# A routed two-layer MoE after attention: one ranking phase moved ahead of an expert, later ranking products moved two places on

## The chip, the cores and the metric

The kernel runs on one core of a Trainium2 chip. The metric is the device time of one execution in microseconds (us). The core has a matrix engine (TensorE, PE in the rows, with its weight loads as PEld), a vector engine (DVE), an activation engine (ACT), GpSimd (POOL) and SyncE (SP), which here mostly issues the weight transfers. Each engine works through its own instructions in program order and waits for the others through semaphores.

## The reference, cut to what matters

Attention over 2 batches, 8 heads and 576 positions gives 1152 rows of 512. They go through a first MoE with 8 experts (top 1, gated), and its output through a second one with 8 experts of exactly 144 rows each. The second is assigned greedily over all logits:

```python
def _moe2_ref(x, w_gate, w1, w2):
    N, D = x.shape
    E = w_gate.shape[1]
    cap = N // E
    logits = x @ w_gate
    flat = logits.flatten()
    order = np.argsort(-flat)
    assigned = -np.ones(N, dtype=np.int64)
    counts = np.zeros(E, dtype=np.int64)
    for idx in order:
        tok, e = (int(idx) // E, int(idx) % E)
        if assigned[tok] >= 0 or counts[e] >= cap:
            continue
        assigned[tok] = e
        counts[e] += 1
    out = np.zeros((N, D), dtype=np.float32)
    for e in range(E):
        mask = assigned == e
        h = np.maximum(x[mask] @ w1[e], 0.0)
        out[mask] = h @ w2[e]
    return out
```

In the attention, the score rows have a maximum subtracted before the exponential. That changes nothing but the range of the numbers.

## The kernel before, in words

**Attention.** A loop over `m` works on one head per turn, several stages of different heads side by side. `ORDER` is a hand-written list of stage names, one list for even and one for odd turns, and sets the order on every engine. `M0` to `M3` make the score pieces from which the row maxima come, `D0` to `D3` take the maxima on DVE (line 488, tile `rm`), `G0` rounds them on ACT (`q_dve0`, line 494), and `G1` uses them on POOL. `TE` copies transposed operands on ACT (line 409), `E0` to `E3` end in the exponentials on ACT (line 536), and `S` and `QS` split operands.

**Experts.** The weights of 16 experts (8 of each MoE) come from HBM in quarters of a 2 MB matrix, issued by SP (line 128) as soon as the expert is known and its buffer is free. Most of them are split into a high f16 part on ACT (line 160) and a low bf16 part on DVE (line 164), so that a product is three matmuls of 16 bit. The layers of the second MoE are `layer1` (lines 1004 to 1006) and `second2` (line 1948). For the second layer, `HALF2` says how many of the 8 row chunks are split; the rest are multiplied as f32. e8 to e15 are the experts of the second MoE in the order in which they fill up.

**Ranking.** That order comes from ranking phases. Phase 0 runs over all rows; phases 1 to 7 (`phases`, a generator) over the rows that are left. A phase puts the maxima into rows by PE transposes (`rows_of`, line 1221) and ACT copies (line 1224), compares on DVE (line 1661) and ACT (line 1659) into tiles `g`, multiplies these on PE (line 1667, behind the start on line 1845), takes from that the rows of the expert that has filled up (`mx`, `BA`, `own`, `O`, `R` on DVE), counts on PE (line 1885), and gets the expert's number into `evi`. `known` makes SP load that number and start the expert's weights. Then `slot_pe` (line 1518) and `choose` give the row numbers `tok`, with which POOL gathers the rows (`xg`, line 1523); `spread` transposes them (line 1543) into `xt`, the expert's input.

**What sets the order there.** `moe2` calls `tick(k)` at 22 places of an expert's two layers, k from 0 to 11 in the first and 12 to 21 in the second, and a script says for each place what goes in: `w` the next step of the ranking, `h` and `l` a high and a low part of the weights that come next, `s` and `t` the two halves of the next spread, `0` and `1` the transposes and output of the expert before (`back2`, line 1964). `FIRST` is e8's script, `THEN` that of all others. Ahead of e8, phase 1 is begun: rows, three steps of compares. `warm(n)` issues n matmuls of 512 columns whose result nobody reads (line 1721).

Of the kernel before, what the change touches and what calls it, by code (L numbers as in the profile page):

```python
# [14 lines left out]
OP = mybir.AluOpType  # L15
AX = mybir.AxisListType
# [5 lines left out]
def tile_attention_moe_moe(ctx: ExitStack, tc: tile.TileContext, q, k, v, s, wg1, w1a, w2a, capacity,  # L22
# [94 lines left out]
    def load_part(i, c):  # L117
        w, k = halves[i]
        t = loaded[i] = place(i)
        e = order[i // 2]  # L120
        src = (w[e:e + 1] if isinstance(e, int) else w[bass.ds(e, 1)]).rearrange("o (c p) f -> p (o c) f", p=P)
        n, f = src.shape[1:]
        t = t.rearrange("p (c f) -> p c f", c=n)
        if i // 2 == E:
            sl = (slice(None), slice(None), slice(c * f // 4, (c + 1) * f // 4))
        else:
            sl = (slice(None), slice(c * n // 4, (c + 1) * n // 4))
        nc.sync.dma_start(t[sl], src[sl])
# [45 lines left out]


    HALF2 = 4
    second_splits = [(2 * E + i, part) for i in range(2 * E) for part in range(HALF2 // 2 if i % 2 else 4) if i != 1]

    def split_next():
        if split_queue:  # L180
# [634 lines left out]
    def some_w(n):  # L815
# [4 lines left out]
    between = gate0()  # L820

    ORDER = [
        "E0 Q E1 K X1 M0 D0 V0 M1 V1 D1 X QE M2 VS XE E3 P0 D2 P1 QS E2 V2 R0 R1 G0 M3 T R2 D3 XG VT TE L LG G1 LV S".split(),
        "E0 VS M0 V0 Q D0 M1 E1 D1 P0 P1 V1 X1 E3 K E2 QE M2 V2 D2 R0 M3 X T R1 G0 LG XE TE R2 D3 QS L S G1 VT XG LV".split(),
    ]
    made = {}
    for m in range(-7, NH + 3):
# [700 lines left out]

    gates = []

    def spread(xg, x=None, k=None, between=(0, 0)):
        if not k:
            gates.append(rw.tile([S2, 2], F32, name="gq", bufs=3))
            nc.vector.tensor_copy(gates[-1], xg[:, :, DM + E])
        x16 = xg.bitcast(F16)
        x = x or mo2["xt"].tile([P, 8, CAP2], F16, name="xt")
        ks = range(2) if k is None else (k,)
        prs = {k: banks[k].tile([P, 512], F32).bitcast(F16)[:, :4 * CAP2].rearrange("p (c q) -> p c q", c=4)
               for k in ks}
        for h in range(2):  # L1540
            for k in ks:
                for c in range(4):
                    nc.tensor.transpose(prs[k][:, c, h * S2:(h + 1) * S2],
                                        x16[:, h, (4 * k + c) * P:(4 * k + c + 1) * P], ident[:S2, :S2])
            if between[h]:
                warm(between[h])
        for k in ks:
            (nc.vector.tensor_copy if k else nc.scalar.copy)(x[:, 4 * k:4 * k + 4], prs[k])
        return x
# [143 lines left out]
    def pop_lo():  # L1693
        if late:
            split_lo(*late.pop(0))
# [142 lines left out]
    def phases():  # L1838
# [3 lines left out]
        for p in range(1, E):  # L1842
# [29 lines left out]
            own = rw.tile([P, CT, E], F32, name="own1")  # L1872
            r = rw.tile([P, CT], F32, name="r1")
            nw = rw.tile([P, CT], F32, name="nw1")
            nc.vector.tensor_tensor(own, pc, BA, OP.mult)
            if not last:
                nc.vector.reduce_sum(nw, BA, axis=AX.X)
            nc.vector.reduce_sum(r, own, axis=AX.X)
            O, R, places = slot_ones(r, BA, Lr[:, :, E], CT, 1)
            in_turn(places)  # L1880
            nc.gpsimd.tensor_add(SL2, SL2, own)
            nc.gpsimd.tensor_add(A, A, BA)
            yield
            for t in range(CT):
                nc.tensor.matmul(cnt2, ones, BA[:, t], start=t == 0, stop=t == CT - 1)
            f, ops = newly_full(p)
# [3 lines left out]
            if not last:  # L1890
# [2 lines left out]
                                                               op0=OP.mult, op1=OP.add),  # L1893
                        lambda: nc.vector.tensor_scalar(pen, fp, -BIG, None, op0=OP.mult),
                        lambda: nc.vector.tensor_tensor(Lo, Lo, c3(pen), OP.add)] + ops
            in_turn(counts, [None] + left)
            known(p)
            if not last:
                m, Bo, Bh, tm = new
            yield  # L1900
# [2 lines left out]
            in_turn(choose(p, f))  # L1903
            chosen.append(p)
            yield

    chk = rp.tile([P, 2, NTT, E], F32, name="chk")
    bad = rp.tile([P, 2, E + 1], F32, name="bad")
# [79 lines left out]
    def moe2(script, first=False):  # L1988
        pend = None
        given.difference_update(range(E, 2 * E))  # L1990
        for e in range(E):
# [21 lines left out]
                    load_next()  # L2013
                    gather_next()

            halved = HALF2 if e else 0
            hs = layer1(mo2, split_ws(i0), XT1.pop(e), CAP2, none, tick, halved)
            pend = (e, second2(i0 + 1, hs, halved, tick), gates[0])
            gates.pop(0)
# [20 lines left out]

    FIRST = "w . lw . . w . w w w w . w . wh l w h st lh wl hll"
    THEN = "w h l h l0 w w . w . h w1l h wl h . w l s tl h l"
    FIRST, THEN = (x.split() for x in (FIRST, THEN))
    next(work)
    pop_lo()
    pop_lo()
    pop_hi()
    warm(WARM2[2])  # L2050
    XT1[0] = spread(xg.pop(0), between=(3, 2))
    next(work)
    next(work)
    next(work)
    pop_hi()
    pop_lo()
    moe2(lambda e, k: (THEN if e else FIRST)[k].strip("."), True)
    assert next(work, None) is None
    bv = nc.values_load(badi[0:1, 0:1], min_val=0, max_val=4 * E)
    with tc.If(bv > 0):  # L2060
        with tc.If(nc.values_load(overi[0:1, E:E + 1], min_val=0, max_val=1) > 0):
            overflown()
        route_all()
        split_queue += second_splits
        given.difference_update(range(E, 2 * E))
        loads += [(i, c) for i in range(2 * E, 4 * E) for c in range(4)]
        order.update({E + e: e for e in range(E)})
        load_next()
        late.clear()
        for _ in range(3):  # L2070
            pop_hi()
        pop_lo()
        XT1[0] = spread(gather(tok[:, 0]))

        def again(e, k):
            if k == 8 and e + 1 < E:
                xg[e + 1] = gather(tok[:, e + 1])
            return THEN[k].strip(".")

        moe2(again)  # L2080
    last_rows()
# [35 lines left out]
```

## Time and profile before

| what | value |
|---|---|
| three executions | 442.37, 442.89 (median), 448.96 us |
| profiled execution | 441.93 us, of which the span of instructions is 440.1 us |
| granted TensorE clock, mean over the span | 0.973 of full |
| busy in the span | PE 396.0, PEld 366.0, DVE 333.6, ACT 261.8, POOL 191.1 us |
| HBM read | 81.42 MB |

Times of rows count from the span's start. The profiled execution is 1.83 us longer than its span, and 0.96 us shorter than the median. A matmul's row is longer than its turn on the engine, since matmuls overlap: its cost is read from start to start.

### The profile page before, as it was taken

The numbers are of one execution on the slowest core, as the hardware profiler recorded it, in microseconds if no ns is written. First come the engines' busy times: TensorE is split into PE (matmuls) and PEld (weight loads), VectorE is DVE, ScalarE is ACT, GpSimd is POOL, SyncE is SP. The second block draws the span as 40 slices with busy tenths as digits, with TensorE's granted clock in tenths as the row PEclk, the third lists the DMA queues.
The fourth block names the chain that finished last, engine by engine and source line by source line (L and its number), as shares of the span: only waits on it lengthen the run. The fifth ranks groups of instructions, "written<-read, shape, count | busy, mean of one in ns | idle before, by whom it ended". The sixth has DMA issues, their size and how long they took to land.

```text
span 440.1 us, 13965 instructions
## 1 busy us (share of the span) xinstructions
PE 396.0 (90%) x5376; PEld 366.0 (83%) x5376; DVE 333.6 (76%) x955; ACT 261.8 (59%) x472; POOL 191.1 (43%) x306
## 2 busy tenths in 40 slices
PE   1679999998878799999999999869989999999994
PEld 1457888886766799999999999738879999999993
DVE  7889999989677377867778894858596878876730
ACT  4448888876482255556565853535476776766641
POOL 4397788875770702142044181522054244244121
PEclk9979999999899999999999999988989999999998
DMA  6797899952987869999999691188999697899511
GB/s 153 168 216 166 181 212 225 224 148 81 311 290 234 298 158 306 384 343 343 335 346 391 99 174 20 29 251 218 356 359 343 200 354 281 242 334 345 171 41 35
DMA packets 94399, 103.04 MB, mean 234 GB/s; under 512 B 56136, under 2 KB 63304, under 8 KB 94323
## 3 DMA queue, kind: packets, MB, share of 16 engines
q1 hardware_dynamic: 88931, 91.85, 71.6%
q0 software_dynamic: 4192, 9.91, 7.3%
q8 instruction: 44, 0.72, 0.7%
q10 hardware_dynamic: 1200, 0.30, 0.3%
q14 instruction: 32, 0.26, 0.2%
HBM read 81.42 MB, written 14.59 MB: 218 GB/s over the span
## 4 chain that ended last, share of the span: by engine, by line
PE 57%; DMA 14%; DVE 13%; issue 6%; ACT 4%; SPq 3%; POOL 2%; POOLq 0%; DVEq 0%; ACTq 0%
PE C L1061 11%; DMA xg<-x2d,tok 7%; PE A L1004 4%; PE A L1005 4%; PE A L1006 4%; PE pog L559 3%; PE C L1948 3%; PE pT L452 3%; DVE wl L164 3%; PE pM L476 2%; PE pE L528 2%; DMA wf<-in_moe_w_dram 2%; PE pE L529 2%; DVE wf L164 2%; PE A L1948 2%
## 5 line engine op out<-in xcount | busy, mean ns | idle before, releaser
L164 DVE TENSOR_TENSOR wl<-wf,wh 128x1024 bf16<-128x1024 f32 x64 | 77.0, 1222 | 22.7 <-ACT wh L160 22.2
L160 ACT ACTIVATE wh<-wf 128x1024 f16<-128x1024 f32 x64 | 65.7, 1050 | 18.5 <-DMA wf<-in_moe_w_dram 10.5
L1005 PE MATMUL A<-xt,wh 128*128 128x144 f16 (+4 forms) x288 | 59.5, 231 | 0.0
L1006 PE MATMUL A<-xt,wl 128*128 128x144 f16 (+4 forms) x288 | 59.5, 231 | 0.0
L1004 PE MATMUL A<-xt,wh 128*128 128x144 f16 (+4 forms) x288 | 59.5, 231 | 0.0
L1061 PE MATMUL C<-h,wf 128*128 128x160 f32 (+7 forms) x544 | 58.3, 269 | 0.0
L1176 POOL DMA_INDIRECT x2d<-xo,tix x14 | 22.9, 1638 | 71.2 <-DVE l L1193 26.5
L1004 PEld LDWEIGHTS <-wh 128*128 128x128 f16 x512 | 50.6, 99 | 2.2 <-PE pM L653 1.6
L1005 PEld LDWEIGHTS <-wh 128*128 128x128 f16 x512 | 50.4, 99 | 1.5 <-issue 1.0
L1006 PEld LDWEIGHTS <-wl 128*128 128x128 bf16 x512 | 50.5, 99 | 0.0
L536 ACT ACTIVATE pf<-pE,XB 128x512 f32<-128x512 f32 (+4 forms) x80 | 36.9, 514 | 10.5 <-PE pE L531 10.3
L414 POOL TENSOR_TENSOR pl<-pf,ph 128x512 f16<-128x512 f32 x30 | 35.6, 1196 | 11.4 <-DVE ph L403 8.8
L1972 POOL DMA_INDIRECT out_dram<-x2f,tok x14 | 16.2, 1160 | 55.4 <-ACT h L1012 26.3
L164 DVE TENSOR_TENSOR wf<-wf,wf 128x1024 bf16<-128x1024 f32 x30 | 35.7, 1218 | 2.6 <-ACT wf L160 2.6
L1523 POOL DMA_INDIRECT xg<-x2d,tok x16 | 24.9, 1556 | 26.3 <-PE A L1221 11.2
L1061 PEld LDWEIGHTS C<-h,wf 128*128 128x128 f32 x256 | 36.2, 190 | 0.0
L488 DVE CUSTOM_DVE_ANT_0 junk<-pM,cb 128x128 f16<-128x128 f32 (+4 forms) x80 | 32.1, 430 | 4.6 <-PE pM L478 3.9
L476 PE MATMUL pM<-al,ar 128*128 128x128 f16 (+2 forms) x96 | 26.5, 317 | 7.1 <-DVE rm L488 6.9
L1948 PE MATMUL C<-h,wf 128*128 128x144 f32 (+1 forms) x312 | 32.6, 260 | 0.0
L160 ACT ACTIVATE wf<-wf 128x1024 f16<-128x1024 f32 x30 | 31.3, 1051 | 0.0
L559 PE MATMUL pog<-vf,pf 128*128 128x65 f32 x180 | 29.1, 284 | 0.0
L1006 PE MATMUL C<-xt,wl 128*128 128x144 f16 x128 | 25.1, 229 | 0.0
(431 smaller groups left out, 1190.0 us busy)
## 6 DMA issues: line engine op xcount, KB each, us to landing
wf<-in_moe_w_dram SPq DMA_DIRECT2D x128, 512.0 KB
xd<-zero SPq DMA_DIRECT2D x18, 257.0 KB
cb<-cumd SPq DMA_DIRECT2D x16, 288.0 KB
x2d<-zero SPq DMA_DIRECT2D x9, 260.5 KB
kf<-in_k_dram SPq DMA_DIRECT2D x16, 128.0 KB
vf<-in_v_dram SPq DMA_DIRECT2D x16, 128.0 KB
qf<-in_q_dram SPq DMA_DIRECT2D x14, 128.0 KB
bl<-al SPq DMA_DIRECT2D x16, 72.0 KB
```

The costliest lines, as they stand in the source:

```text
L160: nc.scalar.activation(hi, src, AF.Copy)
L164: nc.vector.tensor_sub(lo, src, hi)
L414: (nc.gpsimd if ENG[name][i % 2] == "P" else nc.vector).tensor_sub(o, x, y)
L476: nc.tensor.matmul(o, AR[m][:, t * P:(t + 1) * P], AL[m][:, j0:j1], start=True, stop=not diag)
L488: nc.vector.tensor_tensor_reduce(junk[:w, :j1 - j0], o, CB[m][:w, j0:j1], 1.0, r if t == 4 and j0 == 0 else -3e38, OP.add, OP.max, r)
L536: nc.scalar.activation(d, o, AF.Exp, bias=x, scale=2.0 ** -13)
L559: nc.tensor.matmul(o, pf[:, c:c + P], VF[n % 4][:, j, h], start=False, stop=j == t)
L1004: nc.tensor.matmul(ph[:, g], wh[:, c, fs], xt[:, c], start=c == 0, stop=False)
L1005: nc.tensor.matmul(ph[:, g], wh[:, c, fs], xt[:, 4 + c], start=False, stop=False)
L1006: nc.tensor.matmul(ph[:, g], wl[:, c, fs], xt[:, c], start=False, stop=c == 3)
L1061: nc.tensor.matmul(py[:, g], a[:, f, d], b[:, f], start=k == 0, stop=k == len(terms) - 1)
L1948: nc.tensor.matmul(py[:, g], a[:, f, d], b[:, f], start=k == 0, stop=k == len(terms) - 1)
```

## The change

There are five edits.

- In `ORDER`, `G0` goes behind `D3` (and, on even turns, behind `TE`): the maxima are rounded when the last piece is in.
- Phase 1 is carried further ahead of e8's first layer: its products run between the two halves of e8's spread, its count behind them, and `known(1)` ahead of the layer. Its `choose` comes at place 5 of e8, and what prepares phase 2 (`left`) at place 6 instead of together with the count. The matmuls of `warm` around it are 2 and 2 instead of 3 and 2.
- The scripts: e8's phase 2 compares at places 11 and 12 and multiplies at 14 (before: 8 to 10 and 12). e9 has a script of its own, `SECOND`. In `THEN` the products stand at place 10 instead of 8, the count at 13 instead of 11, `choose` at 16 instead of 13, and the next rows at 20 instead of 16.
- e8's second weight matrix is loaded in blocks of rows (128x2x512) instead of blocks of columns (128x8x128).
- e9's second layer isn't split any more: `halved` is 0 for it, as for e8, and its two pieces leave the list of splits.

```diff
-        if i // 2 == E:
+        if i == 2 * E:
             sl = (slice(None), slice(None), slice(c * f // 4, (c + 1) * f // 4))
...
-    second_splits = [(2 * E + i, part) for i in range(2 * E) for part in range(HALF2 // 2 if i % 2 else 4) if i != 1]
+    second_splits = [(2 * E + i, part) for i in range(2 * E) for part in range(HALF2 // 2 if i % 2 else 4) if i not in (1, 3)]
...
-        "E0 Q E1 K X1 M0 D0 V0 M1 V1 D1 X QE M2 VS XE E3 P0 D2 P1 QS E2 V2 R0 R1 G0 M3 T R2 D3 XG VT TE L LG G1 LV S".split(),
-        "E0 VS M0 V0 Q D0 M1 E1 D1 P0 P1 V1 X1 E3 K E2 QE M2 V2 D2 R0 M3 X T R1 G0 LG XE TE R2 D3 QS L S G1 VT XG LV".split(),
+        "E0 Q E1 K X1 M0 D0 V0 M1 V1 D1 X QE M2 VS XE E3 P0 D2 P1 QS E2 V2 R0 R1 M3 T R2 D3 XG VT TE G0 L LG G1 LV S".split(),
+        "E0 VS M0 V0 Q D0 M1 E1 D1 P0 P1 V1 X1 E3 K E2 QE M2 V2 D2 R0 M3 X T R1 LG XE TE R2 D3 G0 QS L S G1 VT XG LV".split(),
...
             if between[h]:
-                warm(between[h])
+                between[h]()
...
-            in_turn(places)
-            nc.gpsimd.tensor_add(SL2, SL2, own)
-            nc.gpsimd.tensor_add(A, A, BA)
-            yield
+            if p == 1:
+                yield
+            else:
+                in_turn(ranked)
+                in_turn(places)
+                kept_ranks()
+                yield
             for t in range(CT):
                 nc.tensor.matmul(cnt2, ones, BA[:, t], start=t == 0, stop=t == CT - 1)
...
-            in_turn(counts, [None] + left)
-            known(p)
+            if p == 1:
+                yield
+                in_turn(counts, ranked)
+                known(p)
+                yield
+                in_turn(places)
+                kept_ranks()
+            else:
+                in_turn(counts, [None] + left)
+                known(p)
...
+            if p == 1:
+                in_turn(left)
+                yield
...
-            halved = HALF2 if e else 0
+            halved = HALF2 if e > 1 else 0
...
-    FIRST = "w . lw . . w . w w w w . w . wh l w h st lh wl hll"
-    THEN = "w h l h l0 w w . w . h w1l h wl h . w l s tl h l"
+    FIRST = "w . l . . w w . . . . www w . wh l h w st wlh wl hll"
+    SECOND = ". . . . 0 w w w . . w 1 h wl h . wl h ls tl wh l"
+    THEN = "w h l h l0 w w . . . wh 1l h wl h . w l s tl wh l"
...
     next(work)
     pop_lo()
     pop_lo()
     pop_hi()
+    for _ in range(3):
+        next(work)
+    pop_lo()
+    pop_hi()
     warm(WARM2[2])
-    XT1[0] = spread(xg.pop(0), between=(3, 2))
+
+    def ranked_first():
+        next(work)
+        warm(2)
+
+    def counted_first():
+        next(work)
+        warm(2)
+
+    XT1[0] = spread(xg.pop(0), between=(ranked_first, counted_first))
     next(work)
-    next(work)
-    next(work)
-    pop_hi()
-    pop_lo()
```

Three places show the moves on an engine. The first is DVE between e8's second and third low part (`wl_84`) and phase 1's maximum `mx`, `BA` and number `evi`; `gq` and `xt` belong to e8's spread, `tot` is the count. Before:

```order
L1504 TENSOR_TENSOR R_5797<-BA_5787,hq_5795 128x40 x2
L164 TENSOR_TENSOR wl_84<-wf_78,wh_83 128x4x256
L1888 TENSOR_TENSOR tot<-tot,px 128x8
L1676 TENSOR_SCALAR full<-tot 128x8
L1892 SCALAR_TENSOR_TENSOR Lm<-nw_5791,Lm 128x5
```

After:

```order
L1871 SCALAR_TENSOR_TENSOR BA_5756<-mx_5754,Bo_5674 128x40
L1548 COPY xt<-A_5715 128x576
L1895 TENSOR_TENSOR tot<-tot,px 128x8
L1875 TENSOR_TENSOR own_5758<-px,BA_5756 128x40
L1676 TENSOR_SCALAR full<-tot 128x8
L1876 TENSOR_REDUCE nw_5760<-BA_5756 128x5
```

The count and the number now stand ahead of the slot tiles `O` and `R` and of e8's fourth low part, not behind them.

The second place is DVE in e8's second layer, behind phase 2's slot tile `R`; `wl_86` is the first low part of e9's first matrix. Before:

```order
L1504 TENSOR_TENSOR R_6036<-BA_6026,hq_6034 128x40 x2
L1888 TENSOR_TENSOR tot<-tot,px 128x8
L1676 TENSOR_SCALAR full<-tot 128x8
L1892 SCALAR_TENSOR_TENSOR Lm<-nw_6030,Lm 128x5
L1677 TENSOR_TENSOR nf<-full 128x8
```

After:

```order
L1504 TENSOR_TENSOR R_6040<-BA_6033,hq_6038 128x40 x2
L164 TENSOR_TENSOR wl_86<-wf_3046,wh_85 128x4x256
L1895 TENSOR_TENSOR tot<-tot,px 128x8
L1676 TENSOR_SCALAR full<-tot 128x8
L1899 SCALAR_TENSOR_TENSOR Lm<-nw_6037,Lm 128x5
```

Phase 2's count, and with it e10's number, now stands behind a split of e9's weights.

The third place is ACT in one attention turn, with the rounding of `rm`, the copies `al` and `ar` of `TE`, and the exponentials `pf` of the next turn. Before:

```order
L494 ACTIVATE rm_159<-rm_159,magic 128x5
L409 ACTIVATE al_140<-pT 128x576
L409 ACTIVATE ar_146<-pT 128x576
L536 ACTIVATE pf_161<-pE,XB 128x512
L536 ACTIVATE pf_161<-pE,XB 128x64
```

After:

```order
L409 ACTIVATE al_140<-pT 128x576
L409 ACTIVATE ar_146<-pT 128x576
L494 ACTIVATE rm_159<-rm_159,magic 128x5
L536 ACTIVATE pf_161<-pE,XB 128x512
L536 ACTIVATE pf_161<-pE,XB 128x64
```

The rounding went from ahead of the two copies to right ahead of the exponentials, and it now waits for the maximum of the last piece.

## Rows read from the trace of the kernel before

**Rows 1.** The page, chain that ended last, by engine.

```profile
PE 57%; DMA 14%; DVE 13%; issue 6%; ACT 4%; SPq 3%; POOL 2%; POOLq 0%; DVEq 0%; ACTq 0%
```

**Rows 2.** The chain in order of time, 280 to 440: start, us, what.

```profile
290.81 4.86 DMA xg<-x2d,tok
295.71 0.43 PE A L1543 x8
296.14 0.65 PE C L1721 x3
...
303.56 0.31 PE px L1518 x5
...
305.38 0.56 PE A L1221 x5
...
307.68 7.46 DMA wf<-in_moe_w_dram
315.25 1.06 ACT wh L160
...
346.96 0.47 PE D L1964 x4
```

**Rows 3.** Timeline of PE, e8 to e11: start, us, line, op, tiles, count.

```profile
297.65 0.28 PE L1004 MATMUL D<-xt,wh 128*128 128x144 f16 x1
...
308.29 0.18 PE L1845 MATMUL px<-tm,part 128*128 128x40 f16 x1
...
309.05 0.37 PE L1948 MATMUL D<-h,wf 128*128 128x144 f32 x1
...
312.45 0.37 PE L1948 MATMUL C<-h,wf 128*128 128x144 f32 x1
...
314.50 0.20 PE L1543 MATMUL A<-ident,xg 72*128 72x72 f16 x1
...
319.01 0.23 PE L1004 MATMUL C<-xt,wh 128*128 128x144 f16 x1
...
338.95 0.23 PE L1004 MATMUL D<-xt,wh 128*128 128x144 f16 x1
...
341.95 0.27 PE L1964 MATMUL D<-identf,y 128*72 128x128 f32 x1
...
343.89 0.18 PE L1845 MATMUL px<-tm,part 128*128 128x40 f16 x1
...
345.19 0.22 PE L1004 MATMUL A<-xt,wh 128*128 128x144 f16 x1
...
355.65 0.23 PE L1004 MATMUL C<-xt,wh 128*128 128x144 f16 x1
```

**Rows 4.** Timeline of DVE, in attention and in e8.

```profile
66.20 0.07 DVE L488 DVE_READ_ACCUMULATOR2_ANT rm<- 64x1 f32 x1
...
105.28 0.07 DVE L488 DVE_READ_ACCUMULATOR2_ANT rm<- 64x1 f32 x1
...
304.15 0.15 DVE L1679 TENSOR_SCALAR evi<-evf 128x1 int32<-128x1 f32 x1
```

**Rows 5.** Windows: stretch, length; busy of PE, PEld, DVE, ACT, POOL; PEclk, DMA, GB/s.

```profile
40.00:65.00 25.00, 25.00 (x367) 21.58 (x366) 24.24 (x86) 20.99 (x49) 19.84 (x25) 1.00 0.89 187
...
293.50:297.00 3.50, 1.29 (x20) 0.93 (x21) 0.73 (x2) 0.94 (x2) 0.29 (x4) 0.98 0.48 117
297.00:300.50 3.50, 3.50 (x52) 2.99 (x49) 3.35 (x7) 2.99 (x4) 0.00 (x0) 0.51 1.16 311
300.50:302.50 2.00, 2.00 (x38) 2.00 (x36) 1.90 (x12) 0.41 (x1) 0.49 (x2) 1.00 1.17 295
```

**Rows 6.** Timeline of ACT in attention; in brackets its idle time before and what ended it.

```profile
64.75 0.30 ACT L494 ACTIVATE rm<-rm,magic 128x5 f32<-128x5 f32 x1
...
66.14 1.42 ACT L536 ACTIVATE pf<-pE,XB 128x512 f32<-128x512 f32 x3
...
107.64 0.65 ACT L409 ACTIVATE xt<-pT 128x576 f16<-128x576 f16 x1 [2.91 <-PE pT L452]
```

More of the change, by code (lines that the diff above doesn't have):

```diff
@@ L1529, in tile_attention_moe_moe, with spread @@
     gates = []
-    def spread(xg, x=None, k=None, between=(0, 0)):
+    def spread(xg, x=None, k=None, between=(None, None)):
         if not k:
@@ L1874, in phases, with kept_ranks @@
             nw = rw.tile([P, CT], F32, name="nw1")
[L1875 to L1878, printed above, removed]
+            ranked = [lambda: nc.vector.tensor_tensor(own, pc, BA, OP.mult),
+                      lambda: last or nc.vector.reduce_sum(nw, BA, axis=AX.X),
+                      lambda: nc.vector.reduce_sum(r, own, axis=AX.X)]
             O, R, places = slot_ones(r, BA, Lr[:, :, E], CT, 1)
-            in_turn(places)
-            nc.gpsimd.tensor_add(SL2, SL2, own)
-            nc.gpsimd.tensor_add(A, A, BA)
-            yield
+            def kept_ranks():
+                nc.gpsimd.tensor_add(SL2, SL2, own)
+                nc.gpsimd.tensor_add(A, A, BA)
+            if p == 1:
[5 more added lines that the diff above has]
+                yield
             for t in range(CT):
@@ L2039, in gather_next @@
                 passed(999)
-    FIRST = "w . lw . . w . w w w w . w . wh l w h st lh wl hll"
-    THEN = "w h l h l0 w w . w . h w1l h wl h . w l s tl h l"
-    FIRST, THEN = (x.split() for x in (FIRST, THEN))
+    FIRST = "w . l . . w w . . . . www w . wh l h w st wlh wl hll"
+    SECOND = ". . . . 0 w w w . . w 1 h wl h . wl h ls tl wh l"
+    THEN = "w h l h l0 w w . . . wh 1l h wl h . w l s tl wh l"
+    SCRIPTS = [x.split() for x in [FIRST, SECOND] + [THEN] * (E - 2)]
     next(work)
@@ L2049, in tile_attention_moe_moe @@
     pop_hi()
+    for _ in range(3):
+        next(work)
+    pop_lo()
+    pop_hi()
     warm(WARM2[2])
-    XT1[0] = spread(xg.pop(0), between=(3, 2))
-    next(work)
-    next(work)
-    next(work)
-    pop_hi()
-    pop_lo()
-    moe2(lambda e, k: (THEN if e else FIRST)[k].strip("."), True)
+    def ranked_first():
[5 more added lines that the diff above has]
+    XT1[0] = spread(xg.pop(0), between=(ranked_first, counted_first))
+    next(work)
+    moe2(lambda e, k: SCRIPTS[e][k].strip("."), True)
     assert next(work, None) is None
@@ L2077, in again @@
                 xg[e + 1] = gather(tok[:, e + 1])
[L2078 removed]
+            return SCRIPTS[-1][k].strip(".")
         moe2(again)
```

## The prediction

> **What bounds the kernel now.** I read the chain of waits first. PE has 57% of it [rows 1], so most of the span is matmuls in sequence, and only a stretch whose chain runs through something else can give much. The reader is to look for such a stretch, and it lies between 290 and 327: the chain goes from e8's gather (the rows land at 290.81 + 4.86 = 295.67) through e8's transposes and small matmuls to a weight transfer of 7.46 us, and then to e9's first high part on ACT at 315.25 [rows 2]. e9's weights are loaded only when phase 1 has found e9, and they come too late.
>
> The timeline of PE gives the price. First layers start at 297.65 (e8), 319.01 (e9), 338.95 (e10) and 355.65 (e11) [rows 3]: an expert takes 21.36, 19.94 and 16.70 us. The chain runs through PE from e10 on, so 16.70 is what PE needs, and the first two are longer by waits. DVE's timeline has e9's number `evi` at 304.15 [rows 4]; the weights are in at 315.15, 11.0 us behind it.
>
> **The change part by part.**
>
> *Phase 1 ahead of e8.* All of phase 1's products, its count and four warming matmuls now stand between e8's gather and e8's first layer; the compares run while PE waits for the gather anyway, so they cost nothing. The prices: eight transposes 0.43; the products from 308.29 to 309.05, 0.76; a warming matmul 0.65 / 3 = 0.22 [rows 2, 3]. The granted clock matters here. The windows show it at 0.98 in 293.5 to 297, when PE was busy for only 1.29 of 3.5 us, then 0.51 up to 300.5, and 1.00 behind that [rows 5]: half rate came behind the wait for the gather and ended while e8's first layer ran. The wait stays, so I take the same times. Then: 295.71 + 0.43 + 0.76 = 296.9; two warming matmuls at half rate 0.87; the other eight transposes 0.43; the count, five matmuls of 8 columns, 0.31 as the like step on line 1518 [rows 2]; two more 0.87. e8's first layer starts at about 299.4, **1.75 later** (at full rate throughout it would be 298.2, 0.55 later).
>
> The trace can't show what the transposes themselves do for the clock, since warming matmuls ran beside them. The Trainium skill (TensorE: Matmul & The Clock Gate, Part 4: PE-mode transpose) says that transposes in that mode don't count as activity for the clock in the way matmuls do. By that rule e8's new start, with fewer warming matmuls and no layer beside the ranking, would stay at half rate for longer, and the sum would be that of the second rival; by the rows it is the one here.
>
> *e8 itself.* I build it from e10's 16.70. In e10 the ranking takes from 343.89 to 345.19, 1.30 where the products alone take 0.76, so 0.54 is a wait for ACT's compares. A whole f32 second layer is 64 half products of (314.50 - 312.45) / 16 = 0.128, 8.2 us. A half split one is 48 products of (341.95 - 338.95) / 48 = 0.0625 and 32 of 0.128, 7.1 us [rows 3]. So an f32 expert without waits is 16.70 - 0.54 + 1.1 = 17.26. e8 has no transposes of an expert before it (2 x 0.47) but a second slot step and a second rows step (0.31 + 0.56) [rows 2], which cancel. The clock is at half until 300.5 [rows 5], 1.1 us of e8, which costs 0.55. e8: 17.8 instead of 21.36, so e9 starts at 317.2, **1.85 earlier**.
>
> What must hold for that: phase 2's products come behind 12 f32 products of e8's second layer (24 halves, 3.1 us), when both compares are done. And e8's second matrix must be in by about 306.5; its rows of 2 KB were asked for at the same time as the columns before, which the f32 products got without a wait. Row blocks I cost at nothing for that reason. If they came later than 306.5, each us would count in full, since the first product now needs all four quarters soon.
>
> *e9's weights.* The number is now some eight small DVE steps (about 0.15 each, as `evi`'s 0.15 [rows 4]) behind the count, near 299.8 instead of 304.15. With the 11.0 us of before, the weights are in at 310.8. Queued behind them: e9's first low part stands on DVE ahead of phase 2's count, and that ahead of e10's number and of the next rows. Phase 2's products end near 310.7 and the slot tiles some 2 us later, so the weights have about 1 us of slack there. The three other splits then fit into the end of e8 and e9's first layer, where each quarter takes PE 1.5 us and a split less.
>
> *e9's second layer in f32* costs PE 1.1 us (above) and takes two high and two low parts off ACT and DVE, which today stand between the compares of phase 3. With weights in time and the products behind the first layer, no wait is left: e9 takes 17.26 instead of 19.94, **2.7 less**. e10 starts at 334.4.
>
> *Products two places later* in e10, e11 and e12: the wait of 0.54 goes in each, **1.6 less**. e13's phase has no compares. The next expert's number comes later in its expert by two places, some 2 us; in e11 the weights have over 3 us between landing and first use, so I cost this at nothing. POOL's gather and SP's load stand behind the same steps and also move by some 2 us with nearly an expert's time to spare.
>
> *Rounding behind D3.* In attention PE is busy 25.0 of 25 us and DVE 24.24 [rows 5]. On ACT the rounding is 0.30 long and the exponentials start at 66.14 [rows 6]; the last maximum is ready at 66.27 [rows 4], so they start at about 66.6, 0.46 later, and on the other turns about 0.30. ACT is busy 20.99 of 25 and has an idle gap in each turn, so I take **nothing**; without this cover it is 0.3 to 0.46 per head. It may be below nothing too, because D3 no longer waits for the rounding.
>
> **The sum**: -1.85 - 2.7 - 1.6 = -6.15. Against the profiled execution, 441.93 - 6.15 = 435.8. The median lies 0.96 above that execution, so I expect a median of about **436.5**.
>
> **The rivals.**
>
> *First: e9 is known early, but its weights aren't there early*, because they queue behind e8's second matrix and the gather. For it: the transfers were near full from 297 on (DMA share 1.16 and 1.17 [rows 5]). Against it: the first expert's transfer was through before e9's was asked for. If they land at 315.15 as before, the first split ends near 317.5, phase 2's count and the next rows follow on DVE, and e9 starts near 320, 1.0 later than before; e9 and the ranking still gain 2.7 + 1.6. That is 441.93 - 3.3 = 438.6, or 439.5 as a median.
>
> *Second: the clock.* If all of e8's first layer ran at half rate, its 96 x 0.0625 = 6.0 us would cost 6.0 more instead of 0.55: 441.93 - 0.7 = 441.2, a median of 442, no change. Against it: PE is nearly without pause from 295.7, as it was when the clock came back in the trace.
>
> *Third, on the slower side: the rounding holds ACT.* It waits for D3 in ACT's queue, and the next turn's exponentials stand behind it. With no cover that is 8 x 0.46 + 8 x 0.30 = 6.1 us. Near the end it is more: D3 is ready only at 105.35 [rows 4], and the idle 2.91 before the copy at 107.64 [rows 6] shows what cover there is; twice that is 5.8. In all up to 11.9, so 441.93 - 6.15 + 11.9 = 447.7. It decides against the change once more than half of that (6.15) reaches PE. The chain through attention has PE in nearly every step, which speaks against it.
>
> *Fourth, better:* full rate sooner at e8 (1.2 + 0.55), D3 free of its wait, a little less elsewhere: 8 to 9 us, a median near 434.
>
> **How the numbers follow.** Forecast (434 to 438.5) 0.58; first rival 0.16; second 0.08; third 0.06; fourth 0.12. The range from 432.8 to 441.8 takes in the fourth, the first and part of the second. Two per cent, about what a measurement of this kernel can tell from no change, is 434.0 and 451.7. Half to all of the fourth lies below 434.0, hence faster 0.12; only a bad third rival reaches 451.7, hence slower 0.04; the same 0.84.
>
> **What would show each step.** In the changed profile: e8's first layer near 299.4, e9's near 317.2, e10's near 334.4, then steps of 16.2; `evi` near 299.8; no wait of ACT for e9's weights beyond 311; half clock ending by 300.5; attention as long as before. I am wrong if e8's start moves by more than 3 us, if e9's first split waits for its transfer beyond 313, or if ACT's wait for D3 turns up as a wait of PE.

## The result, and the profile after

The changed kernel takes **438.75 us** (median of 20 executions, 436.99 to 443.77), the kernel before beside it 443.4 (20 executions, 441.87 to 448.96): a ratio of **0.9892, 95% interval 0.9868 to 0.9916**, 4.65 us less. That is 1.1%, less than the 2% that the prediction took for a clear difference. Forecast were 436.5 and a range of 432.8 to 441.8. One long execution of each kernel (443.77 and 448.96) is left out of the ratio.

The profiled execution of after took 438.96 us with a span of 437.1 and a mean granted clock of 0.970. The timeline of PE has the same first layers as before [rows 3], and a wait in e11's products:

```profile
299.48 0.33 PE L1004 MATMUL D<-xt,wh 128*128 128x144 f16 x1
...
317.56 0.23 PE L1004 MATMUL C<-xt,wh 128*128 128x144 f16 x1
...
334.74 0.23 PE L1004 MATMUL D<-xt,wh 128*128 128x144 f16 x1
...
351.39 0.23 PE L1004 MATMUL C<-xt,wh 128*128 128x144 f16 x1
...
358.21 0.27 PE L1667 MATMUL px<-Bh,g 128*128 128x8 f16 x5
358.84 0.28 PE L1667 MATMUL px<-Bo,g 128*128 128x8 f16 x5 [0.36 <-DVE g L1661]
```

e8, e9, e10 and e11 start 1.83 us later, 1.45, 4.21 and 4.26 us earlier than before. Up to e10 that is the forecast (299.4, 317.2 and 334.4). From there on nothing more is gained.

DVE has the number of e9 at 299.92 (before: 304.15 [rows 4]), and ACT splits e9's first weights at 310.46 without a wait (before: 315.25 [rows 2]). Later in the program, in e13, ACT waits for weights, and a hidden piece `h` queued behind that, and PE for the piece:

```profile
299.92 0.15 DVE L1679 TENSOR_SCALAR evi<-evf 128x1 int32<-128x1 f32 x1
```

```profile
310.46 1.04 ACT L160 ACTIVATE wh<-wf 128x1024 f16<-128x1024 f32 x1
...
391.76 1.06 ACT L160 ACTIVATE wh<-wf 128x1024 f16<-128x1024 f32 x1 [1.93 <-DMA wf<-in_moe_w_dram]
392.72 0.39 ACT L1015 ACTIVATE h<-C 128x288 f32<-128x288 f32 x1
```

```profile
393.17 0.76 PE L1966 MATMUL C<-h,wf 128*128 128x144 f32 x4 [0.39 <-ACT h L1015]
```

The windows of [rows 5] in after:

```profile
40.00:65.00 25.00, 25.00 (x369) 21.57 (x367) 24.33 (x85) 21.30 (x49) 18.31 (x24) 1.00 0.88 183
293.50:297.00 3.50, 1.12 (x31) 1.12 (x32) 3.41 (x6) 3.50 (x5) 0.49 (x4) 0.50 0.53 148
297.00:300.50 3.50, 3.50 (x39) 2.40 (x37) 2.10 (x16) 0.67 (x2) 0.50 (x2) 0.50 0.96 349
300.50:302.50 2.00, 2.00 (x26) 2.00 (x24) 1.86 (x5) 0.25 (x1) 0.00 (x0) 0.70 1.01 341
```

The clock is at half already in the wait for the gather (before: 0.98), and until behind 300.5.

For all kernels of this study the same marks, read from PE's timeline, stand in one table: from the first transpose of e8's spread (the gather has landed) to e8's first layer ("to e8"), then from each expert's first layer to the next, and the whole from the spread to e15. The stages ahead of the spread vary by some us from run to run, as said below, so profiles are compared from there. The names in the first column are runs; a bare e8 to e15 is always an expert.

```
                    to e8   e8     e9     e10    e11    e12    e13    e14   whole
before               1.94  21.36  19.94  16.70  16.70  16.16  15.00  14.97  122.77
after                3.60  18.08  17.18  16.65  16.67  16.12  15.76  15.25  119.31
e11_changed          3.31  17.49  17.18  16.66  16.67  16.12  15.11  17.07  119.61
e1_phase1_inside     1.95  21.27  17.18  16.67  16.66  16.12  15.12  15.20  120.17
e2_old_places        3.34  17.76  18.66  18.13  16.71  16.15  15.01  15.67  121.43
e3_rows_earlier      3.28  18.75  17.35  16.63  16.11  16.02  15.00  16.43  119.57
e4_old_rounding      3.59  18.15  17.17  16.67  16.67  16.12  15.12  16.53  120.02
e5_columns           3.60  18.00  17.18  16.66  16.66  16.12  15.11  16.37  119.70
e6_e9_split          3.48  18.24  18.26  16.93  16.46  16.11  15.12  15.20  119.80
e7_warm_gather       2.48  17.00  17.18  16.66  16.66  16.12  15.11  14.97  116.18
e8_rows_count        3.59  18.76  17.17  16.14  16.14  15.64  15.15  14.97  117.56
e9_best              2.48  18.58  17.86  17.00  16.14  15.64  15.15  16.86  119.71
e10_best_inside      1.94  21.44  17.18  16.54  16.14  15.64  15.15  15.23  119.26
e12_count_later      2.65  18.26  17.18  16.76  16.91  17.40  16.17  16.25  121.58
```

### The profile page after: what moved, and what is told of

It is laid out like the page before. It is cut to its first block, busy times and chain, and to the rows that moved or that the text cites. A ratio compares the mean times of both kernels' runs of the same rounds, so it can differ in the third digit from the quotient of the medians.

```text
span 437.1 us, 13916 instructions
## 1 busy us (share of the span) xinstructions
PE 394.2 (90%) x5359; PEld 364.2 (83%) x5359; DVE 327.0 (75%) x951; ACT 258.4 (59%) x470; POOL 185.9 (43%) x306
## 4 chain that ended last, share of the span: by engine, by line
PE 57%; DMA 14%; DVE 13%; issue 6%; ACT 4%; POOL 2%; SPq 1%; POOLq 0%; ACTq 0%; DVEq 0%
PE C L1061 11%; DMA xg<-x2d,tok 7%; PE C L1966 4%; PE A L1006 4%; PE A L1004 4%; PE A L1005 4%; PE pog L559 3%; PE pT L452 3%; DVE wl L164 2%; PE A L1966 2%; DMA kf<-in_k_dram 2%; PE pM L476 2%; DMA wf<-in_moe_w_dram 2%; DVE wf L164 2%; PE D L1966 2%
## 5 line engine op out<-in xcount | busy, mean ns | idle before, releaser
L164 DVE TENSOR_TENSOR wf<-wf,wf 128x1024 bf16<-128x1024 f32 x28 | 33.4, 1219 | 2.6 <-ACT wf L160 2.6
L1966 PE MATMUL C<-h,wf 128*128 128x144 f16 (+1 forms) x304 | 33.0, 261 | 0.4 <-ACT h L1015 0.4
L1523 POOL DMA_INDIRECT xg<-x2d,tok x16 | 19.8, 1236 | 25.9 <-PE A L1543 7.1
L160 ACT ACTIVATE wf<-wf 128x1024 f16<-128x1024 f32 x28 | 29.3, 1053 | 0.0
L1004 PE MATMUL C<-xt,wh 128*128 128x144 f16 x128 | 24.6, 226 | 0.0
```

The lines of the kernel that those rows point to most:

```text
L160: nc.scalar.activation(hi, src, AF.Copy)
L164: nc.vector.tensor_sub(lo, src, hi)
L1004: nc.tensor.matmul(ph[:, g], wh[:, c, fs], xt[:, c], start=c == 0, stop=False)
L1966: nc.tensor.matmul(py[:, g], a[:, f, d], b[:, f], start=k == 0, stop=k == len(terms) - 1)
```

## The experiments

Each is the changed kernel with the edit shown. They ran in three groups of four, each group on one chip with the kernel before beside it (medians 444.0, 441.35 and 444.67 us), so ratios to the kernel before are what is compared across groups. The intervals are 0.4 to 1% of the time wide (2 to 4 us); terms smaller than that are read from the profiles.

### Phase 1 back inside e8

```diff
-            if p == 1:
+            if p == 0:
...
-    FIRST = "w . l . . w w . . . . www w . wh l h w st wlh wl hll"
+    FIRST = "w . lw . . w . w w w w . w . wh l w h st lh wl hll"
...
-    XT1[0] = spread(xg.pop(0), between=(ranked_first, counted_first))
+    XT1[0] = spread(xg.pop(0), between=(lambda: warm(3), lambda: warm(2)))
```

> The changed kernel with phase 1 put back inside e8 (products at place 0, count at 2, the choice at 5, and phase 2 at its old places); all other edits stay. Theory A, the gain is e9's weights asked for earlier: e8's first layer starts 1.8 us earlier again (297.7), e9's about 2 us later than in the changed kernel (319.5 or later), and since e9 then waits for its first high part as before while its second layer stays f32, e10 starts near 338; the time goes up by about 4, to 442.5 to 443.5. Rival B, the gain of 4.2 us up to e10 comes mostly from e9's second layer not being split (it frees ACT and DVE): then e10 starts within 1.5 us of where the changed kernel has it, and the time is 439 to 440.

The three steps of phase 1 go behind the spread again, too. Ratio 0.9949 (0.9918 to 0.9979), median 441.95, between the times of the two theories. Both had a part. e9's number comes at 303.61 again, its weights are waited for as before, and e8 takes 21.27 us. But e9 takes 17.18 as in the changed kernel:

```profile
314.63 1.06 ACT L160 ACTIVATE wh<-wf 128x1024 f16<-128x1024 f32 x1 [6.01 <-DMA wf<-in_moe_w_dram]
```

```profile
318.38 0.23 PE L1004 MATMUL C<-xt,wh 128*128 128x144 f16 x1
...
335.56 0.23 PE L1004 MATMUL D<-xt,wh 128*128 128x144 f16 x1
```

From the spread to e10 it is 40.40 us, against 43.24 before and 38.86 after. So with weights that come late, the unsplit second layer of e9 with its later products gives 2.84 us alone, and phase 1 ahead adds 1.54. By the ratios it is more: 0.9949 and 0.9892 are 2.5 us apart. The execution profiled here is the shortest of this kernel's twelve, so 1.54 may be too small.

### e9's second layer split again

```diff
-    second_splits = [(2 * E + i, part) for i in range(2 * E) for part in range(HALF2 // 2 if i % 2 else 4) if i not in (1, 3)]
+    second_splits = [(2 * E + i, part) for i in range(2 * E) for part in range(HALF2 // 2 if i % 2 else 4) if i != 1]
...
-            halved = HALF2 if e > 1 else 0
+            halved = HALF2 if e else 0
...
-    SECOND = ". . . . 0 w w w . . w 1 h wl h . wl h ls tl wh l"
+    SECOND = ". h l h l0 w w w . . wh 1l h wl h . wl . s tl wh l"
```

> The changed kernel with half of e9's second layer split again (two high and two low parts more in e9's script), products still at place 10. Theory A, with the weights asked for early the unsplit layer is no longer needed: e9 takes 16.7 instead of 17.2 us, the wait in its products comes back as in e10 (0.5), and the sum is within 0.6 us of the changed kernel. Rival B, the gain in e9 comes from taking the split pieces off ScalarE and VectorE, since the run with phase 1 inside e8 kept e9 at 17.2 us with late weights: then e9 takes 18.5 to 20 us here, and the time goes up by 1.5 to 2.7.

Ratio 0.9891 (0.9846 to 0.9937), that of the changed kernel. e9 takes 18.26 us, between the two theories: its second layer is cheaper on PE, but its products wait 0.93 for compares, and PE waits for a hidden piece that stands on ACT behind a split for which e10's weights are late:

```profile
323.90 1.06 ACT L160 ACTIVATE wh<-wf 128x1024 f16<-128x1024 f32 x1 [2.70 <-DMA wf<-in_moe_w_dram]
```

```profile
325.31 0.76 PE L1966 MATMUL C<-h,wf 128*128 128x144 f32 x4 [0.92 <-ACT h L1015]
```

From the spread to e10 it is 39.98 us. Phase 1 ahead without the unsplit layer gives 3.26 us, the unsplit layer without phase 1 ahead 2.84, both together 4.38: the two remove partly the same wait.

### The old places of products, count, choice and rows

```diff
-    SECOND = ". . . . 0 w w w . . w 1 h wl h . wl h ls tl wh l"
-    THEN = "w h l h l0 w w . . . wh 1l h wl h . w l s tl wh l"
+    SECOND = "w . . . 0 w w . w . . w1 h wl h . wl h ls tl h l"
+    THEN = "w h l h l0 w w . w . h w1l h wl h . w l s tl h l"
```

> The changed kernel with the products at place 8, the count at 11, the choice at 13 and the next rows at 16 from e9 on, as before; phase 1 stays ahead of e8. Theory A, the later places gain nothing in e10 to e12, since there a wait of 0.36 to 0.5 us for a compare on VectorE took the place of the one removed, and they lose 1.0 us in e13 and e14, where the weights of the expert after come later: 437.6 to 438.2, 0.5 to 1.2 us faster. Rival B, the prediction's step: the old places bring back 0.54 us of waiting in each of e10, e11 and e12, and 440 to 440.5.

Ratio 0.9864 (0.9815 to 0.9914): by the time it can't be told from the changed kernel. In the profile e11 and e12 take 16.71 and 16.15, as with the later places (16.67 and 16.12); rival B's half a us is not there. e13 and e14 together take 30.68, 0.33 less than after. e9 and e10 take 1.5 us more each: e9's count waits for what stands close ahead of it here, phase 3's maxima on DVE (`mx` to `own`), and e10's first layer for the second half of its input:

```profile
324.45 0.27 PE L1892 MATMUL px<-BA,ones 128*128 128x8 f16 x5 [0.80 <-DVE own L1875]
...
335.84 0.22 PE L1005 MATMUL D<-xt,wh 128*128 128x144 f16 x1 [1.27 <-DVE xt L1548]
```

That second half is copied at 335.33, 1.9 us behind the transposes that it reads. In the kernel before, which has the same places in e10, the copy comes 0.2 us behind them. So the loss in e10 isn't shown to come from the places, and its cause stays open.

### The rows earlier

```diff
-    SECOND = ". . . . 0 w w w . . w 1 h wl h . wl h ls tl wh l"
-    THEN = "w h l h l0 w w . . . wh 1l h wl h . w l s tl wh l"
+    SECOND = ". . . . 0 w w w . . w 1 h wl h . wl wh ls tl h l"
+    THEN = "w h l h l0 w w . . . wh 1l h wl h . w wl s tl h l"
```

> The changed kernel with the next rows at place 17 instead of 20 in e9's script and that of the later experts; products, count and choice stay where the change has them. Theory A, the third VectorE compare is late because the rows are copied on ScalarE only behind the start of the next expert, and the first splits, the hidden pieces and the compare stand behind that copy: with the rows three places earlier the wait in the products of e10, e11 and e12 (0.36 to 0.5 us each) goes, and the time is 437.3 to 437.9, some 1.1 us faster. Rival B, the compare is late because of the low parts ahead of it in VectorE's queue, whatever the rows do: the wait stays and the time is 438.5 to 439.2.

Ratio 0.9846 (0.9798 to 0.9894). The wait is gone, so theory A holds for the place of it. In after, e11's ACT and DVE rows are these (e11 starts at 351.39):

```profile
351.43 0.77 ACT L1224 ACTIVATE rowb<-A 128x384 f32<-128x384 f32 x2 [1.81 <-PE C L1966]
352.08 1.06 ACT L160 ACTIVATE wh<-wf 128x1024 f16<-128x1024 f32 x1
```

```profile
353.17 1.23 DVE L164 TENSOR_TENSOR wl<-wf,wh 128x1024 bf16<-128x1024 f32 x1 [2.16 <-ACT wh L160]
...
355.60 2.35 DVE L164 TENSOR_TENSOR wf<-wf,wf 128x1024 bf16<-128x1024 f32 x2
...
358.23 0.55 DVE L1661 TENSOR_SCALAR g<-rowb,m 128x640 f16<-128x640 f32 x1
```

The rows step at place 20 puts ACT's copy `rowb` at the start of the expert. A high part, a low part, two compares and two more low parts queue behind it in turn, and the third compare ends at 358.78, after the products have begun. With the rows at place 17 (e11 starts at 353.27) ACT copies ahead of the expert, and the last products follow without a gap:

```profile
349.99 0.77 ACT L1224 ACTIVATE rowb<-A 128x384 f32<-128x384 f32 x2 [1.41 <-PE A L1221]
```

```profile
358.96 0.55 DVE L1661 TENSOR_SCALAR g<-rowb,m 128x640 f16<-128x640 f32 x1
```

```profile
360.09 0.27 PE L1667 MATMUL px<-Bh,g 128*128 128x8 f16 x5
360.21 0.27 PE L1667 MATMUL px<-Bo,g 128*128 128x8 f16 x5
360.34 0.27 PE L1667 MATMUL px<-Bh,g 128*128 128x8 f16 x5
```

From the first compare product to the next other matmul on PE, e11's 25 products take 1.19 us before, 1.14 after and 0.62 here. Not all of it reaches the end: e11 gains 0.56, but e10 loses 0.43 of it ahead of its slot step and e12 as much ahead of its count.

### The count one place earlier, and one place later

```diff
-    THEN = "w h l h l0 w w . . . wh 1l h wl h . w l s tl wh l"
+    THEN = "w h l h l0 w w . . . wh 1 wh l hl . w wl s tl h l"
```

> The changed kernel with the next rows at place 17 and the count at 12 instead of 13, ahead of a low part instead of behind it, from e9 on. Theory A, two terms: the wait in the products of e10, e11 and e12 goes (0.52 each, as with the rows alone), and the numbers of the experts are known 1.2 us earlier, so that the weights are there when e13 and e14 split them and the waits of TensorE for a hidden piece in e13 and e14 (0.4 to 1.1) go: e13 15.0 and e14 15.0 to 15.3 us, the time 437 or less. Rival B, the count now waits on TensorE for the maxima (0.5 to 0.8 in each expert, as where the products stood at 8 in e9), and nothing is gained: 438.5 or more.

Ratio 0.9816 (0.978 to 0.9852), the lowest of all. e10, e11 and e12 take 16.14, 16.14 and 15.64, each 0.5 us less, and e13 and e14 together 30.12 where after has 31.01. ACT waits for no weights in these two. Theory A holds. `SECOND` was changed in the same way.

The other way, with the rows left at 20 (`SECOND` likewise):

```diff
-    THEN = "w h l h l0 w w . . . wh 1l h wl h . w l s tl wh l"
+    THEN = "w h l h l0 w w . . . wh 1l h l wh . . wl s tl wh l"
```

> The changed kernel with the count one place later still (14 instead of 13) from e9 on, the choice at 17. Theory A, the weights of the next expert are a full step behind their number, and the margin in e13 and e14 is gone: each place later (0.75 us and a low part) shows there nearly in full, e13 and e14 together take 31.5 us or more, the time is 1 to 2 us above the changed kernel's. Rival B, the waits in e13 and e14 come from transfers that are slow now and then, whatever the count: the two together 30.1 to 31.0 us, no difference in time.

Ratio 0.9966 (0.9944 to 0.9988); the intervals of this and of the changed kernel beside it (0.9879, 0.9836 to 0.9921) don't overlap. e12, e13 and e14 each have the chain that after showed in e13, here e12's:

```profile
376.20 1.06 ACT L160 ACTIVATE wh<-wf 128x1024 f16<-128x1024 f32 x1 [2.31 <-DMA wf<-in_moe_w_dram]
```

```profile
377.60 1.51 PE L1966 MATMUL D<-h,wf 128*128 128x144 f32 x16 [0.93 <-ACT h L1015]
```

e12 takes 17.40 us and e13 16.17, 1.3 and 1.1 more than in the changed kernel beside it, and e14 16.25. The medians differ by 4.3 us, more than the 1 to 2 expected; the two profiles differ by 2.0, and the profiled execution was the shortest of this kernel's twelve. The time and the new wait in e12 speak for theory A, with an amount that was too small. Its other sign doesn't: e13 and e14 together take 32.42 us, but 32.18 in the changed kernel beside it, too, where the same chain stands in e14:

```profile
406.87 1.06 ACT L160 ACTIVATE wh<-wf 128x1024 f16<-128x1024 f32 x1 [2.95 <-DMA wf<-in_moe_w_dram]
```

```profile
408.28 1.92 PE L1966 MATMUL D<-h,wf 128*128 128x144 f32 x19 [1.58 <-ACT h L1015]
```

The profiles together show more. With the count at 13 (eight profiles) or 14 (this one), ACT waits for weights in e13 or e14 in every one; with the count at 11 or 12 (five) in none. But PE waits behind that for 0.39 to 1.58 us in only five of the eight with the count at 13, and e13 and e14 together take from 30.08 to 32.18. So rival B has a part: the late count takes the margin, and what that costs differs from run to run.

### The rounding as before

The edit puts back both lists of `ORDER`.

> The changed kernel with the stage order of before in attention (the maxima rounded ahead of the last piece). Theory A, attention is 0.2 to 0.5 us longer with the late rounding, as the last first layers start that much later in the changed kernel up to the gather of e8: 438.3 to 438.6. Rival B, the third rival in its small form, a cover that is partly gone: 1 us or more back, under 437.8. Rival C, the late rounding frees the last maximum of its wait: then the old order is slower, 439.5 or more.

Ratio 0.9895 (0.9846 to 0.9944), that of the changed kernel. The profiles tell more: from the first matmul on line 609 to the first on line 699, a stretch of attention at full clock, the old order takes 42.66 us, and the kernel before as well; after, and ten of the other eleven runs, take 42.60 or 42.61. In after and here these matmuls are:

```profile
59.95 0.52 PE L609 MATMUL pT<-wgh,xt 128*128 128x8 f16 x15
...
102.55 0.18 PE L699 MATMUL pog<-OH,before 128*128 128x40 f16 x1
```

```profile
59.77 0.52 PE L609 MATMUL pT<-wgh,xt 128*128 128x8 f16 x15
...
102.43 0.18 PE L699 MATMUL pog<-OH,before 128*128 128x40 f16 x1
```

(The eleventh, with phase 1 inside and all else improved, has 42.82.) Over this stretch, in which PE has no pause, rounding behind the last piece is worth 0.05 us, and none of the three theories' amounts is there: what theory A read as 0.2 to 0.5 us lies within the differences between runs.

Right behind the stretch PE does pause, and there the order shows. PE waits for `cnt`, which stands behind the last maximum on DVE; these are the waits before, here and in after:

```profile
105.52 0.19 PE L562 MATMUL pog<-vh,ph 128*128 128x65 f16 x1 [1.71 <-DVE cnt L782]
```

```profile
106.26 0.19 PE L562 MATMUL pog<-vh,ph 128*128 128x65 f16 x1 [1.70 <-DVE cnt L782]
```

```profile
105.70 0.19 PE L562 MATMUL pog<-vh,ph 128*128 128x65 f16 x1 [1.03 <-DVE cnt L782]
```

From the first matmul on line 699 that is 3.83 us in both kernels with the old order, and 3.15 or 3.16 in all twelve profiles with the late rounding. So rival C has a part, 0.68 us. DVE takes its steps in another order there, and two small ones ahead of `cnt` (`gg`) last 0.75 and 1.04 us with the old order and 0.38 and 0.77 in after; why isn't shown. Nor is it shown how much of the 0.68 us reaches the end: from that matmul to e8's spread it is 194.02 and 193.88 us with the old order, and from 190.71 to 195.68 with the late one.

### Blocks of columns

```diff
-        if i == 2 * E:
+        if i // 2 == E:
```

> The changed kernel with e8's second weight matrix loaded in blocks of columns again. Theory A, the prediction's step: the form of the blocks costs nothing, e8 takes 18.1 us as in the changed kernel, and the time stays within 1 us of it. Rival B, blocks of columns hold the queue longer (2 KB rows became 512-byte pieces): e9's first weights, asked for at 299.9 and split from 310.46, come later by more than 0.5 us and e9's first layer starts later than 21.7 us behind the landing of the gather. Rival C, columns are better, since the first f32 products need one quarter alone: e8 is shorter by some tenths.

Ratio 0.9892 (0.9858 to 0.9926). e8 takes 18.00 us, and from e9's number to its first split it is 10.68 us. The two profiles of the changed kernel have 9.92 and 10.54 there, and the run with the old rounding, which doesn't touch this place, has 11.43. Theory A holds: no cost is seen, within such differences.

### More warming in the wait for the gather

```diff
-    WARM2 = (4, 5, 5)
+    WARM2 = (4, 5, 14)
```

> The changed kernel with 14 instead of 5 warming matmuls ahead of e8's spread, in the wait for the gather. Theory A, the idle wait of TensorE ahead of the gather is what lets the clock fall: with it filled the granted clock is full from the landing on, e8's first layer starts 2.4 instead of 3.6 us behind the landing, its first half takes 3.0 to 3.3 instead of 4.07 us, and the time falls by about 2, to 436.5 to 437.2. Rival B, the transposes and small products of the ranking hold the clock down whatever ran ahead of them: the first layer still starts at half rate, and the time is 438.5 to 439.2. Rival C, the matmuls run past the landing of the gather at half rate: e8's spread starts up to 1 us late, 439.5.

Ratio 0.9862 (0.9821 to 0.9904). The profile agrees with theory A. Its windows are the rows of phase 1, the 14 warming matmuls, the spread with the ranking, and the two halves of e8's first layer:

```profile
286.30:287.40 1.10, 1.09 (x5) 1.06 (x6) 0.36 (x3) 0.53 (x1) 0.00 (x0) 0.50 1.04 360
287.40:292.60 5.20, 5.20 (x16) 1.97 (x14) 4.47 (x6) 4.86 (x8) 2.58 (x5) 0.56 0.69 200
292.60:295.10 2.50, 2.50 (x57) 1.80 (x55) 1.47 (x7) 1.32 (x2) 0.00 (x0) 1.00 0.94 356
295.10:298.10 3.00, 2.96 (x48) 2.93 (x47) 2.93 (x17) 0.43 (x2) 0.50 (x2) 1.00 0.97 337
298.10:301.30 3.20, 3.20 (x57) 3.20 (x55) 2.00 (x12) 0.82 (x2) 1.41 (x2) 1.00 1.02 373
```

The transposes and products of the ranking run at 1.00, not 0.50, the layer's first half takes 3.00 instead of 4.07 us, and e9 starts 19.48 us behind the spread, 2.2 earlier than in after and 1.3 earlier than in the other profile of the changed kernel. The three profiles with 14 or 11 warming matmuls (this one and the two of the next group) have 1.00 from the start of the spread for 7 us; all eleven with 5 have half rate in some of that time. The Trainium skill (TensorE: Matmul & The Clock Gate, Part 1, "HAM oscillation") says that matmuls in bursts with waits for a DMA between them start at half rate again; the 0.50 of after and the 1.00 here agree. Its remark that transposes don't count in the way matmuls do (Part 4) can't be tested here, since matmuls run beside them in every run. Rival C has a part: from the gather's issue to its landing it is 4.46 us in after and 4.89 in the other profile, and here the spread starts 5.26 us behind the issue at 287.43, so the matmuls held it up by some 0.4 to 0.8 us. Part of the gain was so spent, and this profile is of the shortest of six executions; the ratio is 0.0030 below that of the changed kernel, 1.3 us, with intervals that overlap.

### Rows, count and warming together, with phase 1 ahead and inside

The edits are those of the count one place earlier, and `WARM2 = (4, 5, 11)`; the second run has phase 1 inside e8 as well.

> The changed kernel with the rows at place 17 and the count at 12 ahead of a low part (as in the run on rows and count) and with 11 instead of 5 warming matmuls in the wait for the gather. Theory A, the two gains are in different places and add up: e8's first layer starts 2.5 us behind the landing and at full rate, e10 to e12 are 0.5 us shorter each, e13 and e14 together 30.1 us; from the start of e8's spread to the end 131 to 131.5 us (the changed kernel 134.8), the ratio to the kernel before 0.976 to 0.981. Rival B, with e8's layer 2 us earlier the weights of e9 and e10 are now what is late, and e8 and e9 take the 2 us back: 133 us or more from the spread on, ratio 0.982 or more.

> The same with phase 1 back inside e8. Theory A, phase 1 ahead is worth 1.5 us or more also when e9 is unsplit and the clock is full: e9's weights are asked for some 4 us later, e9's first layer starts 21 us or more behind the spread, and the time is 1.5 to 3 us above that of the kernel with phase 1 ahead. Rival B, what phase 1 ahead gains in e9's weights it pays back at e8's start, and with the clock full the two are within 0.7 us.

> The changed kernel itself, as the yardstick for the runs beside it: ratio 0.987 to 0.992 to the kernel before; from the start of e8's spread to the end 134.5 to 135.5 us, with e13 and e14 together anywhere between 30.1 and 31.7 us, as the weights of e14 and e15 arrive.

The ratios are 0.9829 (0.9794 to 0.9865), 0.9909 (0.9877 to 0.994) and, for the changed kernel beside them, 0.9879. That yardstick has 135.1 us from the spread to PE's end, as expected, but 32.18 in e13 and e14, above the 31.7 expected. The first kernel is no better than rows and count alone (0.9816). Its profile fell on the longest of its six executions, 440.71 us, has 135.2 us from the spread to PE's end, and shows what rival B said: e8's first layer ran at full rate, but e9's weights, asked for at 300.54, were split only at 313.95, and the time went back in e8, e9 and e10. The chain, and PE's wait at the end of it:

```profile
303.19 10.66 DMA wf<-in_moe_w_dram
313.95 1.06 ACT wh L160
315.04 1.22 DVE wl L164
316.27 0.08 DVE tot L1895
```

```profile
316.39 0.31 PE L1518 MATMUL px<-R,O 128*72 128x16 f16 x5 [1.07 <-DVE tot L1895]
```

With phase 1 inside, the median is 3.35 us higher (439.95 and 436.6), so phase 1 ahead is worth its place in this form too, as theory A of that run had it; the two profiles alone would not show it (119.71 and 119.26 in the table).

## Why the forecast was right, and where not

**Phase 1 ahead and e9's layer** came out as worked. To e8 it is 1.66 us more (1.75 forecast), e9's number comes at 299.92 (299.8), the first split at 310.46 (310.8), e9 takes 17.18 us (17.26), and from the spread to e10 the gain is 4.38 us (4.55). What the runs with phase 1 inside and with e9 split add is which edit does what: the prediction gave the 2.7 us in e9 the condition "with weights in time", and with phase 1 inside e9 takes 17.18 us with weights as late as before. So the early number, which comes 4.2 us sooner, adds only 1.54 us by the profiles (2.5 by the ratios) to what e9's unsplit layer gives by itself.

**The first rival** has its mechanism, with a size that changes from run to run. The windows show that e9's weights now meet a full queue: before, the transfers idle in part between 304 and 308, and after they don't.

```profile
304.00:308.00 4.00, 4.00 (x58) 3.99 (x56) 2.86 (x15) 2.20 (x5) 1.81 (x2) 1.00 0.44 128
```

```profile
304.00:308.00 4.00, 4.00 (x58) 4.00 (x56) 1.77 (x11) 0.67 (x3) 2.16 (x3) 1.00 1.00 390
```

Behind e8's second matrix, e9's weights take from 9.92 to 13.80 us from their number to the first split in the eleven profiles with phase 1 ahead (11.02 to 11.29 in the three with it inside). The prediction took the 11.0 of before as fixed. In the two profiles of the changed kernel, 10.54 and 9.92, ACT was busy up to the split, so the weights may have landed earlier. In the slowest case (13.80, in the run with the rows earlier) the split comes 17.48 us behind the spread's start, where after has 14.58 and the run with phase 1 inside 19.47, so part of the gain goes and part stays.

**The clock** cost 1.07 us in e8's first layer in the profile of after (its first half took 4.07 instead of 3.00) where 0.55 was forecast. "The wait stays, so I take the same times" is the step that was off there: the fall came before the landing and not behind it. In the other profile of the same kernel (spread at 295.15) it came behind, as forecast, and the half took 3.48:

```profile
293.65:295.15 1.50, 0.00 (x0) 0.00 (x1) 1.50 (x4) 1.50 (x3) 0.00 (x0) 1.00 0.48 117
296.35:298.75 2.40, 2.40 (x20) 1.35 (x19) 1.43 (x10) 0.64 (x1) 0.24 (x1) 0.50 1.04 356
```

The second rival, half rate through all of the layer, came in neither.

**Products two places later** is the step that failed: 1.6 us were forecast, and e10 to e12 gained 0.12 together. The wait before was indeed for ACT's compares, which ended last: in e11 at 361.70, DVE's at 361.35, and the products ended at 361.90.

```profile
360.16 1.54 ACT L1659 ACTIVATE g<-rowb,m 128x640 f16<-128x640 f32 x2
```

```profile
360.80 0.55 DVE L1661 TENSOR_SCALAR g<-rowb,m 128x640 f16<-128x640 f32 x1
```

But the edit moved the rows step too, from 16 to 20, and the prediction gave that move no price. It delays DVE's third compare, and a wait of 0.52 took the place of 0.57. The two runs with the rows at place 17 and phase 1 ahead, without and with the earlier count, show it gone.

**"The next expert's number comes later ... I cost this at nothing"** failed too. "Over 3 us between landing and first use" was read in e11. Before, e13 has no compares and is 1.2 us shorter than e12, and there the slack is used up: e13 and e14 together take 31.0 and 32.2 us in the two profiles of the changed kernel, 29.97 before. With the count at 12 none of three profiles has ACT waiting for weights from e12 on; with it at 14 the loss is in e12, too. (e14's 16.86 in `e9_best` is another wait, 2.01 us for the second half of its own input, like that of e10 in the run with the old places; its cause stays open.)

**Rounding and row blocks** were costed at nothing, and cost nothing that is seen. The third rival's wait is there on ACT (2.19 us for D3 in after, at 104.88), but PE's wait there ends with DVE's `cnt`. The fourth rival's "D3 free of its wait" has a small counterpart, the 0.68 us ahead of `cnt`.

The sum: from the spread to e15 the profile has 3.46 us less, of which e8 to e10's start give 4.38, e10 to e12 0.12, and e13 and e14 take 1.04 back. The forecast was 6.15, and the missing 2.69 are the two steps that failed (1.48 and 1.04) and 0.17 up to e10. The two profiled executions differ by 2.97 and the medians by 4.65: the profiled execution of before was 1.5 us below its median and that of after 0.2 above. So the median came nearer to its forecast (2.25 us off) than the profiled execution (435.8 forecast, 438.96 measured), and that part is luck. Why the share ahead of the spread differs from run to run is not settled: the spread starts between 291.75 and 297.44 in the fourteen profiles, and no run was aimed at that.

## What to carry to other kernels

When a step is moved in a written order, price every step that moves along with it, at the queue that it joins: here a row copy put at the head of an expert made a wait as long as the one that the edit removed. Slack is to be read at the shortest stage that uses it, not at the typical one. A wait for a transfer that must be kept can be filled with matmuls that nobody reads; here that was worth having, as a dense layer follows, and the gain stayed only where what came next wasn't a transfer already late.

## What was not expected of the hardware

e9's first weights took from 9.92 to 13.80 us from their number to the first split at a DMA share near 1.0, in four of the five profiles above 12 us with edits that lie behind that path (old places, rows earlier, e9 split, rows and count), and e14 of one and the same kernel took 15.25 and 17.07 us. One profile of a kernel whose weights arrive just in time doesn't show its typical time. And the granted clock could be brought to 1.00 for e8's start by matmuls that themselves ran at 0.56 on average.
